# Cosine attention with a cosine MLP on one core: another order for the AV matmuls, a second DMA queue at the start, larger weight loads, and a refitted DMA model in the planner

## The chip, the cores and the metric

The kernel runs on one core of a Trainium2 chip. The metric is the device time of one execution in microseconds (us). Before the change the median of three runs was 438.87 us (437.8 to 439.41). The span in a profile is about 1.8 us shorter than the time of the same run.

Names used below: PE is the matmul engine, ACT the engine of exp, cosine and logarithm, DVE the vector engine, POOL the general engine, SP the engine that only issues DMAs. A bank is a piece of the memory in which PE adds up its results. A load lands when its last data have arrived. The granted clock is the share of PE's full speed that the profile records.

## The reference, cut to what matters

```python
# q, k, v: 8 batches x 12 heads x 448 x 64, float32; tau 0.1
q_n = q / (norm(q) + 1e-6);  k_n = k / (norm(k) + 1e-6)
attn = softmax(q_n @ k_n.T / tau)
x = (attn @ v) -> [3584, 768]           # heads side by side
h = x @ w_in                            # 768 x 2048, "M1" below
out = (h * cos(h)) @ w_out              # 2048 x 768, "M2" below
```

## The kernel before

Two heads make a pair. A batch has 6 pairs, a unit is 3 pairs, so there are 48 pairs, 16 units and 8 batches. In each pair PE forms scores (SC), ACT takes their exponential (PX), PE multiplies by v (AV), DVE divides. After six pairs M1 of the batch runs (96 matmuls of 448 columns), ACT takes the cosine (by a sine with an offset), DVE multiplies (gT), and M2 of that batch is left over as a reserve: its matmuls are placed one by one into PE's waits during the attention of the next batch. Where there is nothing to place, filler matmuls on zeros keep PE's clock up.

The order of the instructions on each engine is not written by hand. The program lists all operations with costs and dependencies, and a planner plays them through a model of the engines and of the DMA, tries 12 settings, and fixes each engine's order at build time. At run time each engine executes its list strictly in order. So a wrong number in the planner's model does no harm to the result; it gives an order that fits the chip badly.

The AV matmuls of a pair, before. `AVv[:, a]` are two banks, one for each head `a`; four chunks `c` of keys are added up in one target:

```python
def av(e, a):
    for x in range(NJ):                      # 4 groups of 112 queries
        k = a * S + NP * x
        for c in range(NJ):                  # 4 chunks, same target
            t = e.matmul(AVv[:, a, DV*x : DV*x + n], PXv[j][:, c, k : k + 128],
                         vav[i][:, NJ*(2*p + a) + c, 0:n], start=(c == 0), stop=(c == NJ - 1))
for a in range(2):                           # head after head
    P.op("PE", lambda e, a=a: av(e, a), ..., cost=NJ * NJ * 0.0324, ...)
```

The planner's choice between the attention's next group (at time `s`) and a waiting M2 matmul (at time `t`). `hold` is one of the settings that are tried, 0.1 or 0.2 us:

```python
if s is None or switched(t, o) < s - self.hold:
    s, c = t, (t, o, fill)                   # place M2 here
```

The planner's DMA model gives each load a bulk time and, where several queues are busy, shares the engines in proportion to a packet time:

```python
dma(eng, ..., "load u%d p%d", bulk = 0.82 per pair,  packet 0.055)   # q, k
dma("SP", ..., "load v",      bulk = 2.4,            packet 0.055)
dma("POOL", ..., "W1", 4 loads, bulk = 4.2 each,     packet 0.09)
dma("POOL", ..., "W2", 4 loads, bulk = 4.2 each,     packet 0.13)
```

## Time and profile before

| what | value |
|---|---|
| time | 438.87 us |
| span of the profile | 436.6 us |
| PE busy (filler included) | 97% |
| M1 of batch 0 starts | 37.84 us |
| M1 of batch 1 starts | 95.16 us |
| M1 of batches 2 to 5 start | 148.42, 196.88, 245.35, 293.81 us, every 48.47 us |
| last matmul starts | 432.03 us |

The starts of M1 are read from single matmuls in the trace. They cut the run into stages. The Trainium skill, "Perfetto Trace Analysis", says at its start that matmul busy time is a bad measure of how near a kernel is to its limit, because matmuls are pipelined. Here too the share misleads, if for other reasons: 97% includes 66 filler matmuls, and the first stages have waits that the share does not show.

These are the head, the DMA slices, the chain's share by engine, the AV group, and the issues of W1 from the page of the kernel before. A group has line, engine, operation, output from input, shapes, count, then busy us and mean ns of one (which includes the latency), then the idle time before it.

```profile
span 436.6 us, 8807 instructions
PE 423.0 (97%) x3774; PEld 230.6 (53%) x3774; DVE 211.8 (49%) x295; ACT 266.3 (61%) x320; POOL 191.6 (44%) x119
DMA  8999999899838296747948493848758101210222
...
PE 86%; ACT 5%; POOL 3%; DVE 2%; DMA 2%; SPq 1%; issue 0%; ACTq 0%; POOLq 0%
...
L782 PE MATMUL AV<-va,PX 112*128 112x65 bf16 x1536 | 57.2, 193 | 1.1 <-ACT PX L765 0.8
...
W<-in_moe_w_in_dram POOLq DMA_DIRECT2D x4, 768.0 KB, 12.1
```

The chain is PE for 86% of the span. L782 are the AV matmuls, 57.2 us for 48 pairs. The DMA is busy for 80% or more in each of the first eleven of forty slices, that is for the first 120 us.

PE's timeline (start, length, line, operation, count, idle time before) in the stage after M1 of batch 0 of the kernel before:

```profile
58.39 0.55 PE L760 MATMUL SC<-qkT 64*128 64x448 bf16 x4
58.87 2.12 PE L874 MATMUL PO<-W,gT 128*128 128x384 bf16 x12
60.83 0.54 PE L909 MATMUL PO<-zt 128*128 128x448 bf16 x2
61.84 0.36 PE L760 MATMUL SC<-qkT 64*128 64x448 bf16 x2 [0.47 <-ACT PX L765]
...
66.17 0.55 PE L909 MATMUL PO<-zt 128*128 128x448 bf16 x2
66.56 0.81 PE L874 MATMUL PO<-W,gT 128*128 128x384 bf16 x4
```

From 60.83 to 66.56 us there is no M2 (PO<-W,gT): PE runs scores and filler (L909). Further below this stretch is called the hole. The last W2 load landed at 60.87 us, and the planner had placed M2 after 65.20 us because its model expected the landing then. (Times that the planner expected are read from it when the kernel is built.)

### The profile page before, as it was taken

What the parts mean: (1) busy time and instruction counts of PE and PEld (TensorE: products, weight loads), DVE (VectorE), ACT (ScalarE), POOL (GpSimd) and SP (SyncE); (2) the same over time, 40 slices, a digit from 0 to 9 for tenths busy, and PEclk for the clock granted to TensorE, in tenths of its full rate; (3) what the DMA queues carried; (4) which work ended last, traced back from release to release, by engine and by line L of the source; (5) the groups of instructions that cost most, each with busy time, mean ns of one, the idle gap of its engine ahead of it and who ended that gap; (6) DMA issues with size and microseconds to landing.
All of it is one profiled execution on the core that took longest, in us unless ns stands there. A gap on an engine that the chain in (4) does not pass through costs nothing.

```text
span 436.6 us, 8807 instructions
## 1 busy us (share of the span) xinstructions
PE 423.0 (97%) x3774; PEld 230.6 (53%) x3774; DVE 211.8 (49%) x295; ACT 266.3 (61%) x320; POOL 191.6 (44%) x119
## 2 busy tenths in 40 slices
PE   8789989999999999999999999999999999999996
PEld 3455536555555555555555555555555555555663
DVE  4775644555752269233853268333852343244321
ACT  4886577774777646775487747774577647734000
POOL 0994347857594137910695048911695000000000
PEclk9999999999999999999999999999999999999999
DMA  8999999899838296747948493848758101210222
GB/s 211 247 230 209 239 244 196 196 211 249 224 80 163 62 263 158 135 99 187 240 64 153 114 270 80 167 112 200 180 101 146 46 0 48 69 38 2 73 74 72
DMA packets 95975, 63.87 MB, mean 146 GB/s; under 512 B 54976, under 2 KB 92352, under 8 KB 95936
## 3 DMA queue, kind: packets, MB, share of 16 engines
q1 hardware_dynamic: 90688, 57.02, 57.3%
q0 software_dynamic: 5248, 6.29, 8.3%
q8 instruction: 30, 0.49, 0.5%
q14 instruction: 9, 0.07, 0.1%
HBM read 45.61 MB, written 11.01 MB: 130 GB/s over the span
## 4 chain that ended last, share of the span: by engine, by line
PE 86%; ACT 5%; POOL 3%; DVE 2%; DMA 2%; SPq 1%; issue 0%; ACTq 0%; POOLq 0%
PE PO L874 30%; PE SC L823 20%; PE AV L823 12%; PE AV L782 11%; PE SC L760 9%; ACT PX L765 3%; PE SC L874 2%; DMA raw<-in_q_dram 2%; POOL qks L720 1%; POOL sq L694 1%; DVE n L701 1%; ACT cosb L837 1%; ACT sq L690 1%; PE AV L874 1%; ACT L613 1%; SPq L647 1%
## 5 line engine op out<-in xcount | busy, mean ns | idle before, releaser
L765 ACT ACTIVATE PX<-SC 112x896 bf16<-112x896 f32 x192 | 165.2, 914 | 44.5 <-PE SC L760 43.3
L874 PE MATMUL PO<-W,gT 128*128 128x384 bf16 x816 | 150.2, 326 | 0.0
L694 POOL TENSOR_TENSOR sq<-raw 112x1024 bf16<-112x1024 f32 x41 | 76.7, 1894 | 95.5 <-DMA raw<-in_q_dram 95.5
L874 PEld LDWEIGHTS PO<-W,gT 128*128 128x128 bf16 x816 | 72.9, 98 | 59.2 <-issue 13.0
L720 POOL TENSOR_TENSOR qks<-raw,rn 112x1024 bf16<-112x1024 f32 x47 | 88.3, 1902 | 23.3 <-ACT rn L712 23.2
L823 PE MATMUL SC<-xT,W 128*128 128x448 bf16 x480 | 95.4, 352 | 0.8 <-DVE gT L839 0.5
L839 DVE TENSOR_TENSOR gT<-SC,cosb 128x896 bf16<-128x896 f32 x40 | 43.6, 1091 | 59.5 <-ACT cosb L837 58.9
L837 ACT ACTIVATE cosb<-SC,cst 128x896 f32<-128x896 f32 x40 | 40.2, 1007 | 48.6 <-PE SC L823 46.2
L823 PEld LDWEIGHTS SC<-xT,W 128*128 128x128 bf16 x480 | 46.6, 98 | 43.8 <-issue 0.8
L701 DVE TENSOR_REDUCE n<-sq 112x16 f32<-112x1024 bf16 (+1 forms) x49 | 58.0, 1190 | 16.5 <-ACT sq L690 9.4
L782 PEld LDWEIGHTS AV<-va,PX 112*128 112x128 bf16 x1536 | 51.9, 97 | 15.9 <-issue 11.2
L823 PE MATMUL AV<-xT,W 128*128 128x448 bf16 x288 | 58.7, 352 | 0.1
L760 PE MATMUL SC<-qkT 64*128 64x448 bf16 x384 | 55.0, 355 | 3.8 <-ACT PX L765 1.4
L782 PE MATMUL AV<-va,PX 112*128 112x65 bf16 x1536 | 57.2, 193 | 1.1 <-ACT PX L765 0.8
L881 DVE COPY osb<-PO 128x384 f32<-128x384 f32 x51 | 28.1, 552 | 34.7 <-PE PO L874 34.7
L837 ACT ACTIVATE cosb<-AV,cst 128x896 f32<-128x896 f32 x24 | 24.2, 1007 | 33.1 <-PE AV L823 32.7
L791 DVE RECIPROCAL rcp<-AV 112x8 f32<-112x8 f32 x48 | 9.9, 206 | 67.7 <-PE AV L782 67.6
L823 PEld LDWEIGHTS AV<-xT,W 128*128 128x128 bf16 x288 | 28.0, 98 | 26.2 <-issue 0.5
L839 DVE TENSOR_TENSOR gT<-AV,cosb 128x896 bf16<-128x896 f32 x24 | 26.2, 1091 | 18.3 <-ACT cosb L837 17.9
L792 DVE TENSOR_TENSOR xs<-AV,rcp 112x512 bf16<-112x512 f32 x48 | 33.2, 691 | 2.0
L668 POOL CAST va<-vin 112x1536 bf16<-112x1536 f32 x14 | 20.5, 1462 | 26.1 <-PE AV L782 24.2
L760 PEld LDWEIGHTS SC<-qkT 64*128 64x128 bf16 x384 | 12.9, 93 | 34.9 <-ACT PX L765 17.5
(34 smaller groups left out, 130.9 us busy)
## 6 DMA issues: line engine op xcount, KB each, us to landing
vin<-in_v_dram SPq DMA_DIRECT2D x16, 672.0 KB, 10.4
raw<-in_k_dram SPq DMA_DIRECT2D x13, 672.0 KB, 6.8
raw<-in_q_dram SPq DMA_DIRECT2D x13, 672.0 KB, 8.7
W<-in_moe_w_in_dram POOLq DMA_DIRECT2D x4, 768.0 KB, 12.1
W<-in_moe_w_out_dram POOLq DMA_DIRECT2D x4, 768.0 KB, 19.2
out_dram<-osb SPq DMA_DIRECT2D x8, 336.0 KB, 3.1
out_dram<-osb SPq DMA_DIRECT2D x8, 288.0 KB, 2.7
raw<-in_k_dram SPq DMA_DIRECT2D x9, 224.0 KB, 8.2
```

Source lines behind the costliest of these rows:

```text
L694: pool(lambda e, x=x, y=y: e.tensor_tensor(y, x, x, ALU.mult), src_, dst, 0.1 + n * 1.78e-3, label="sq%d.%d" % (u, p))
L701: dve(lambda e, w=w: e.tensor_reduce(out=n2v[i][:, 2 * p : 2 * p + 2, w], in_=sqv[p][:, :, w, :], axis=mybir.AxisListType.X, op=ALU.add), ...
L720: f = lambda e, s0=s0, s1=s1: e.tensor_tensor(qksv[i][:, p, s0:s1, :, :].rearrange("p s h d -> p h s d"), rawv[i][:, h, s0:s1, :], bass.AP ...
L760: t = e.matmul(SCv[z][:, a, 0:S], qkT[k].ap()[r, NP * c : NP * c + 128], qkT[k].ap()[r, S : 2 * S], start=True, stop=True)
L765: act(lambda e: e.activation(PXv[j][:, c, 0 : 2 * S].rearrange("p (a s) -> p a s", a=2), SCv[z][0:NP, :, 0:S], ACT.Exp, scale=1.0 / TAU), ...
L782: t = e.matmul(AVv[:, a, DV * x : DV * x + n], PXv[j][:, c, k : k + 128], vav[i][:, NJ * (2 * p + a) + c, 0:n], start=(c == 0), stop=(c == ...
L792: dve(lambda e: e.tensor_tensor(xsv[y].rearrange("p x h d -> p h x d"), AXv[:, :, :, 0:D], bass.AP(rcp[y], 0, [[NS, NP], [NJ, 2], [1, NJ], ...
L823: t = e.matmul(ph[:, a, 0:S], W1v[:, c, 128 * n : 128 * n + 128], xTv[b % 2][:, c, :], start=(c == 0), stop=(c == NKC - 1))
L837: act(lambda e, ph=ph, cz=cz: e.activation(cosv[cz], ph[:, :, 0:S], ACT.Sin, bias=cst.ap()[:, 0:1], scale=1.0), names(gi) + ["cst0"], [("c ...
L839: dve(lambda e, ph=ph, cz=cz, gi=gi: e.tensor_tensor(gTv[:, 2 * gi : 2 * gi + 2, S * (b % 2) : S * (b % 2) + S], ph[:, :, 0:S], cosv[cz], ...
L874: r = e.matmul(po[:, 0:HW], gTv[:, y, col : col + 128], W2v[:, y, HW * hf : HW * hf + HW], start=(y == 0), stop=(y == NF - 1))
L881: dve(lambda e, po=po, o=o, hf=hf: e.tensor_copy(osb[o].ap()[:, HW * hf : HW * hf + HW], po[:, 0:HW]), keys, [("osb", o, hf)], HW, label=" ...
```

## The change

Its intent: the matmuls of AV should not wait for the accumulation before them; q, k and v of the first unit should arrive earlier; W1 should cost less DMA time; unit 5's load and norms should not delay batch 1; the planner should know the true landings. The diff, cut to its core (left out among others: new issue times for the weight loads, and the table load on ACT now behind the first issues of q):

```diff
-    "sq": ["AD", "A", "A", "P", "P", "P"],          # who squares: A = ACT, P = POOL, D = DVE
-    "scale": ["D", "P", "P", "P", "P", "P"],
+    "sq": ["AD", "A", "P", "P", "P", "P"],
+    "scale": ["DD", "P", "P", "P", "P", "P"],       # first pair by halves
...
+    MIXED = 0.9                                     # in the DMA model
-            turn = sum(o.pkt for o in run)
+            turn = sum(o.pkt for o in run) * (self.MIXED if len(run) > 1 else 1.0)
...
+            eng = "ACT" if u in HALF and x == (1,) else "SP"      # HALF = (0,): q of unit 0
-                "raw...", 0.82 * (p1 - p0) * len(x), ..., 0.055)
+                "raw...", 0.95 * (p1 - p0) * len(x), ..., 0.068)
...
+        views = (TPv, POv if apart else TPv)        # first pair: halves turned in two banks
...
-        def av(e, a):
-            for x in range(NJ):
-                for c in range(NJ):
+        def av(e, x0):
+            for x in range(x0, x0 + 2):
+                for c in range(NJ):
+                    for a in range(2):              # heads, so banks, alternate
...
-    NQ = 4                          # W1 bulk 4.2, packet 0.09; W2 bulk 4.2, packet 0.13
+    NQ1, NQ2 = 2, 4                 # W1 bulk 15.2 / 2, packet 0.079; W2 bulk 15.2 / 4, packet 0.119
...
-        if u == 3 and p == 1:
-            load(5, 0, UP)
+        if u == 3 and p == 2:
+            for x in range(UP):
+                load(5, x, x + 1)                   # after the store of pair 8's x
...
+            if g in DEFER:                          # DEFER = (2 * PB,): unit 5's norms after M1
+                norms(g // UP + 1, 0)
...                                                  # the last store: two queues, SP and ACT
```

Alternating heads is allowed because the two heads lie in two banks. The Trainium skill, "PSUM — Partial Sum Buffer", The four PSUM rules, says that the first matmul of an accumulation clears the written-bits of the whole bank, in the partitions that it writes; two sums begun in turns in one bank would spoil each other.

More of the change, by code (lines that the diff above doesn't have):

```diff
@@ L309, in transfer @@
                     continue
-                turn = sum(h[0].pkt for h in run)
+                turn = sum(h[0].pkt for h in run) * (self.MIXED if len(run) > 1 else 1.0)
                 step = min([h[2] * turn / h[0].pkt for h in run] + [stop - clock[0]])
@@ L517, in bass_cosine_attention__then__act_gcu_kernel @@
     NO = 4
-    DUE = (-20.0, 8.0, 12.0, 16.0, 20.0, 24.0, 28.0, 32.0)
+    DEFER = (2 * PB,)
+    VDVE = (0, 1)
+    HALF = (0,)
+    DUE = (-20.0, 10.0, 20.0, 24.0, 28.0, 32.0)
     LAG = 1
@@ L573, in bass_cosine_attention__then__act_gcu_kernel @@
     TPv = PO2.ap().bitcast(BF16)
+    POv = PO.ap().bitcast(BF16)
     vav = [t.ap().rearrange("p (x d) -> p x d", d=DV) for t in va]
@@ L635, in bass_cosine_attention__then__act_gcu_kernel @@
         pool(lambda e, i=i: e.memset(PXv[i][:, :, 2 * S :], 0.0), (), [("PX", i, c) for c in range(NJ)], 0.2, label="pad")
-    table(EXPSET)
     def src(t, u, h0, nh):
@@ L640, in src, with load @@
         return bass.AP(t.tensor, (b * NH + hb) * S * D, [[NJ * D, NP], [S * D, nh], [1, NJ * D]])
-    pooled, loads = [None], []
-    def load(u, p0, p1, apart=False, eng="SP", behind=None):
+    pooled, loads, quick = [None], [], []
+    def load(u, p0, p1, apart=False):
         i = u % 2
@@ L650, in load, with load_v @@
         for x in ((0,), (1,)) if apart else ((0, 1),):
-            behind = pooled[0] if eng == "POOL" else loads[-1] if loads else None
+            eng = "ACT" if u in HALF and x == (1,) else "SP"
+            behind = quick[-1] if eng == "ACT" and quick else None if eng == "ACT" or not loads else loads[-1]
             dma(eng, [f[y] for y in x], (), [("raw", i, p, y) for p in range(p0, p1) for y in x],
-                "raw%d_%d_%s%s" % (i, p0, x, eng), 0.82 * (p1 - p0) * len(x), "load u%d p%d" % (u, p0), behind, 0.055)
-            loads.append(P.ops[-1])
-            if eng == "POOL":
-                pooled[0] = P.ops[-1]
-    def load_v(u, eng="SP"):
-        i = u % 2
-        before = loads[-1] if loads and eng == "SP" else None
-        loads.append(dma(eng, [lambda e: e.dma_start(vin[i].ap().rearrange("p (h c) -> p h c", h=UH), src(v, u, 0, UH))],
-            (), [("vin", i)], "vin%d%s" % (i, eng), 2.4, "load v u%d" % u, pooled[0] if eng == "POOL" else before, 0.055))
-        if eng == "POOL":
-            pooled[0] = P.ops[-1]
+                "raw%d_%d_%s%s" % (i, p0, x, eng), 0.95 * (p1 - p0) * len(x), "load u%d p%d" % (u, p0), behind, 0.068)
+            (quick if eng == "ACT" else loads).append(P.ops[-1])
+    def load_v(u):
+        i = u % 2
+        loads.append(dma("SP", [lambda e: e.dma_start(vin[i].ap().rearrange("p (h c) -> p h c", h=UH), src(v, u, 0, UH))],
+            (), [("vin", i)], "vin%d" % i, 2.85, "load v u%d" % u, loads[-1], 0.068))
     def copy_v(u):
@@ L668, in copy_v @@
         f = lambda e: e.tensor_copy(vav[i][:, :, 0:D], vinv[i])
-        if u < 2:
+        if u in VDVE:
             dve(lambda e: e.tensor_reduce(
@@ L676, in halves @@
     def halves(parts):
-        if len(parts) == 1 or parts[0] == parts[1]:
-            return [(parts[0], (0, 1))]
+        if len(parts) == 1:
+            return [(parts, (0, 1))]
         return [(parts[0], (0,)), (parts[1], (1,))]
@@ L739, in transposes, with half @@
             return
-        def half(e, s0, s1):
+        views = (TPv, POv if apart else TPv)
+        keys = (("TP", 0), "PO" if apart else ("TP", 1))
+        def half(e, s0, s1, view):
             for s in range(s0, s1):
-                r = e.transpose(TPv[:, NP * s : NP * s + NP], qksv[i][:, p, s, :, :], ident.ap())
+                r = e.transpose(view[:, NP * s : NP * s + NP], qksv[i][:, p, s, :, :], ident.ap())
             return r
         for t in range(2):
-            P.op("PE", lambda e, t=t: half(e, NJ * t, NJ * t + NJ), [("qks", i, p, t), "ident"],
-                 [("TP", t)], cost=NJ * 0.0487, mode="F", label="TP%d" % g)
+            P.op("PE", lambda e, t=t: half(e, NJ * t, NJ * t + NJ, views[t]), [("qks", i, p, t), "ident"],
+                 [keys[t]], cost=NJ * 0.0487, mode="F", label="TP%d" % g)
         for t in ((0,), (1,)) if apart else ((0, 1),):
             w = slice(S * t[0], S * t[-1] + S)
-            dve(lambda e, w=w: e.tensor_copy(qkT[j].ap()[:, w], TPv[:, w]), [("TP", z) for z in t],
+            dve(lambda e, w=w, view=views[t[-1]]: e.tensor_copy(qkT[j].ap()[:, w], view[:, w]), [keys[z] for z in t],
                 [("qkT", j, z) for z in t], len(t) * S / 2, label="qkT%d" % g)
@@ L776, in attend @@
         i, b, n = u % 2, g // PB, D + 1
-        def av(e, a):
-            for x in range(NJ):
-                k = a * S + NP * x
+        def av(e, x0):
+            for x in range(x0, x0 + 2):
                 for c in range(NJ):
-                    t = e.matmul(AVv[:, a, DV * x : DV * x + n], PXv[j][:, c, k : k + 128],
-                                 vav[i][:, NJ * (2 * p + a) + c, 0:n], start=(c == 0), stop=(c == NJ - 1))
+                    for a in range(2):
+                        k = a * S + NP * x
+                        t = e.matmul(AVv[:, a, DV * x : DV * x + n], PXv[j][:, c, k : k + 128],
+                                     vav[i][:, NJ * (2 * p + a) + c, 0:n], start=(c == 0), stop=(c == NJ - 1))
             return t
         P.group = len(P.ops)
-        for a in range(2):
-            P.op("PE", lambda e, a=a: av(e, a), [("va", i)] + [("PX", j, c) for c in range(NJ)], ["AV"],
-                 cost=NJ * NJ * 0.0324, mode="F", label="AV%d" % g)
+        for x0 in range(0, NJ, 2):
+            P.op("PE", lambda e, x0=x0: av(e, x0), [("va", i)] + [("PX", j, c) for c in range(NJ)], ["AV"],
+                 cost=NJ * NJ * 0.0300, mode="F", label="AV%d" % g)
         P.group = None
@@ L825, in f @@
                 return t
-            P.op("PE", f, [("W1", n // 4)] + [("xT", b % 2, c) for c in range(c0, c1)], names(gi), cost=(c1 - c0) * MM,
+            P.op("PE", f, [("W1", n * NQ1 // NF)] + [("xT", b % 2, c) for c in range(c0, c1)], names(gi), cost=(c1 - c0) * MM,
                  mode="F", label="M1 %d.%d" % (b, n))
@@ L876, in go @@
                     return r
-                P.op("PE", go, [("W2", f // 4)] + sorted({("gT", x, y // 2) for y in range(f, f + step) for x in par}),
+                P.op("PE", go, [("W2", f * NQ2 // NF)] + sorted({("gT", x, y // 2) for y in range(f, f + step) for x in par}),
                      keys, cost=step * MH, mode="F", label="M2 %d" % t, stream="B")
@@ L882, in m2_emit @@
                 keys, [("osb", o, hf)], HW, label="osb%d" % t)
-            if hf == 1:
-                sg = segments(t)
+            sg = segments(t)
+            if t == B * S // 128 - 1:
+                for x, (p0, cnt, row) in enumerate(sg):
+                    w = slice(HW * hf, HW * hf + HW)
+                    q = ("SP", "ACT")[x % 2 if hf else 0]
+                    dma(q, [lambda e, p0=p0, cnt=cnt, row=row, o=o, w=w: e.dma_start(
+                        bass.AP(out.tensor, row * DM + w.start, [[NJ * DM, cnt], [1, HW]]), osb[o].ap()[p0 : p0 + cnt, w])],
+                        [("osb", o, hf)], [], "last%s" % q, 0.6, "out%d" % t, None, 0.14)
+            elif hf == 1:
                 dma("SP", [lambda e, p0=p0, cnt=cnt, row=row, o=o: e.dma_start(
@@ L896, in load_w1 @@
     def load_w1(x):
-        w = FF // NQ
+        w = FF // NQ1
         pooled[0] = dma("POOL", [lambda e: e.dma_start(
             W1v[:, :, w * x : w * x + w], bass.AP(moe_w_in.tensor, w * x, [[FF, 128], [128 * FF, NKC], [1, w]]))],
-            (), [("W1", x)], "W1_%d" % x, 4.2, "W1.%d" % x, pooled[0], 0.09, 1000.0 + DUE[x])
+            (), [("W1", x)], "W1_%d" % x, 15.2 / NQ1, "W1.%d" % x, pooled[0], 0.079, 1000.0 + DUE[x])
     def load_w2(x):
-        w = NF // NQ
+        w = NF // NQ2
         pooled[0] = dma("POOL", [lambda e: e.dma_start(
             W2v[:, w * x : w * x + w, :], moe_w_out[128 * w * x : 128 * w * (x + 1), :].rearrange("(f p) n -> p f n", p=128))],
-            (), [("W2", x)], "W2_%d" % x, 4.2, "W2.%d" % x, pooled[0], 0.13, 1000.0 + DUE[4 + x])
+            (), [("W2", x)], "W2_%d" % x, 15.2 / NQ2, "W2.%d" % x, pooled[0], 0.119, 1000.0 + DUE[NQ1 + x])
     zero = dve(lambda e: e.memset(zt.ap(), 0.0), (), ["zt"], S)
@@ L912, in bass_cosine_attention__then__act_gcu_kernel @@
     for g in range(PB):
-        load(g // UP, g % UP, g % UP + 1, g == 0)
+        load(g // UP, g % UP, g % UP + 1, g == 0 or g // UP in HALF)
         if g % UP == UP - 1:
             load_v(g // UP)
+    table(EXPSET)
+    for y in quick:
+        P.order_only(y, P.ops[-1])
     def find(label):
@@ L943, in pair @@
         u, p = g // UP, g % UP
-        if p == 0 and u >= 2 and u + 1 < NU:
+        if p == 0 and u >= 2 and u + 1 < NU and g not in DEFER:
             norms(u + 1, 0)
@@ L953, in pair @@
                 load_v(4)
-        if u == 3 and p == 1:
-            load(5, 0, UP)
+        if u == 3 and p == 2:
+            for x in range(UP):
+                load(5, x, x + 1)
+            P.order_only(find("X8"), P.ops[-3])
             load_v(5)
@@ L960, in pair @@
             grouped(transposes, g + 1)
-        if BYPE <= g + 3 < NG:
+        if BYPE <= g + 3 < NG and g not in DEFER:
             transposes(g + 3)
@@ L965, in bass_cosine_attention__then__act_gcu_kernel @@
     norms(0, 0)
-    transposes(0)
+    transposes(0, True)
     norms(0, 1)
@@ L969, in bass_cosine_attention__then__act_gcu_kernel @@
     P.order_only(find("scale0.0"), find("red0.1"))
+    for y in [o for o in P.ops if o.label == "qkT0"]:
+        P.order_only(y, find("red0.1"))
     load_w1(0)
@@ L978, in bass_cosine_attention__then__act_gcu_kernel @@
         load(2, p, p + 1)
-    load_w1(2)
-    load_w1(3)
     load_w2(0)
@@ L984, in bass_cosine_attention__then__act_gcu_kernel @@
     load(3, 0, UP)
-    after(P.ops[-1], find("W1.3"))
+    after(P.ops[-1], find("W1.%d" % (NQ1 - 1)))
     load_v(2)
@@ L1007, in bass_cosine_attention__then__act_gcu_kernel @@
             m1(points[g])
+            if g in DEFER:
+                norms(g // UP + 1, 0)
+                transposes(g + 3)
             first = [o for o in P.ops[first:] if o.eng == "PE"][0]
@@ L1023, in bass_cosine_attention__then__act_gcu_kernel @@
     P.arrange()
-    P.emit(nc, ["out%d" % o for o in range(NO)])
+    P.emit(nc, ["out%d" % o for o in range(NO)] + ["lastSP", "lastACT"])
     ctx.close()
```

## The prediction

> What bounds the kernel now. The page of the profile gives PE 97% busy, but part of that is filler (L909). In the chain of waits six batches from 148.6 us on repeat every 48.4 us (148.58, 197.04, 245.51, 293.98, 342.44 us) with almost no piece that is not PE. So from about 116 us to 432 us PE is the limit. Before that it is not. The slices show DMA at 80 to 99% for about 98 us.
>
> Three stages before the steady part, from PE's timeline:
> - 0 to 37.8 us, attention of batch 0. The chain of waits runs through q's landing (9.82 us), a square on ACT (9.84 to 10.9), then POOL without a pause from 11.5 to 24.6 us.
> - 37.8 to 58.4 us, first half of the MLP of batch 0: 96 matmuls x 0.189 = 18.1 us of work in 20.6 us.
> - 58.4 to 95.2 us, attention of batch 1 and M2 of batch 0: by my count about 28 us of PE work in 36.8 us. Between 60.8 and 66.6 us PE runs pairs of score matmuls and filler, and waits for ACT. Yet the last W2 load had landed at 60.87 us (DMA issues with landings). M2 was placed later because the planner's old model expects W2 later: 4.2 x (1 + 0.055/0.13) = 6.0 us per contended load, where the trace shows about 5.4.
>
> What the change does:
> 1. AV order. Starts of single matmuls in the trace: 32 to 33 ns inside an accumulation of four, 29 ns at each change of target. The Trainium skill, "TensorE: Matmul & The Clock Gate", Back-to-back issue gap, gives N/2.4 + 2.5 = 29.6 ns for N = 65 and no wait for accumulating onto the same address; the trace has that wait, about 3.4 ns. Alternating heads alternates banks, so all should be near 29.5. 24 x 3.4 ns = 0.08 us a pair, 3.9 us for 48 pairs, about 3.4 us on the critical path.
> 2. Start. The second square leaves ACT for POOL, idle until 11.5 us; ln and rn come about 0.7 us earlier; one W1 issue (0.8 us) leaves POOL's chain. 1 to 2 us at the start of M1. q of pairs on ACT's queue shares the same 16 engines (the skill, "Trainium Kernel Development and Optimization", Key Constraints), so it saves only issue time, below 0.5 us.
> 3. W1 in two loads doubles its packets. Packets of 1024 bytes took 97 ns, of W2's 1536 bytes 135 ns: 10.5 against 11.4 bytes/ns. My estimate: 1.5 us less DMA time before W2 lands.
> 4. The refit (5.4 us per contended load: 3.8 x (1 + 0.068/0.119) x 0.9) puts M2 into the hole at 61 to 66 us: 3 to 4 us. With 2 and 3, M1 of batch 1 starts at 89.5 instead of 95.2 us.
> 5. Later unit 5 and deferred norms take a 0.95 us square and a 1.2 us reduce out of the chain at 90 to 93 us: about 0.5 us net.
> 6. The last store split over two queues: 0.5 us of the 4.2 us after the last matmul.
>
> Sum: 5.7 + 3.0 (AV after 95 us) + 0.5 + 0.5 = 9.7 us; I take off a tenth for reordering losses. Predicted 430.0 us, range 426.0 to 435.0. Chances: faster by over 2% 0.50, within 2% 0.48, slower 0.02.
>
> Right if: AV groups of 32 take 0.95 us; batch period 47.9 us; filler at 61 to 66 us gone; M1 of batch 1 at about 90 us.
>
> Wrong if: 29 ns cannot be sustained with a weight load for each matmul; unit 3's norms (POOL scale until 79 us) keep batch 1 late; POOL's added square delays its chain; the plan meets other landings than it assumes.

## The result, and the profile after

The changed kernel took 433.01 us (median of four runs, 432.25 to 434.07) against 438.9 us of the kernel before. The ratio is 0.9871, with a 95% interval from 0.9841 to 0.9901. A ratio here is the mean time of one kernel's fast runs over that of the other's in the same rounds, so it isn't quite the ratio of the medians. The time is inside the predicted range and within 2%. The outputs are right.

A second measurement of the same kernel (a_again below) gave 435.09 us and 0.9893. It was run at another time. The medians of the kernel before were within 0.6 us (438.77 to 439.3), its single runs between 437.38 and 441.79 us. So the 2 us between the two medians of the changed kernel need a reason, and one is shown below.

The lines of the page after that answer to those above:

```profile
span 430.4 us, 8767 instructions
PE 417.9 (97%) x3756; PEld 225.6 (52%) x3756; DVE 213.2 (50%) x297; ACT 264.5 (61%) x319; POOL 192.7 (45%) x118
...
PE 81%; ACT 6%; DMA 6%; POOL 4%; issue 1%; DVE 1%; SPq 1%; ACTq 0%
...
L785 PE MATMUL AV<-va,PX 112*128 112x65 bf16 x1536 | 54.7, 193 | 0.8 <-ACT PX L767 0.8
...
W<-in_moe_w_in_dram POOLq DMA_DIRECT2D x2, 1536.0 KB, 14.9
```

AV fell from 57.2 to 54.7 us, and W1 comes in two loads of double size. The chain is less of PE (81% for 86%) and more of DMA (6% for 2%). Three pieces of the chain of the changed kernel, in order of time (start, length, what), show where the DMA got into it:

```profile
113.57 7.50 POOL qks L719 x4
...
123.24 8.12 DMA raw<-in_q_dram
131.43 3.75 POOL sq L693 x2
```

Loads of q and k and what POOL makes of them now decide something in batch 1. In the kernel before, the chain from 116.50 us to the end of that batch is PE alone.

The stages, from the starts of M1 and of the last matmul, with the number of M2 matmuls that lie in each:

| stage | before, us | M2 | after, us | M2 | difference |
|---|---|---|---|---|---|
| up to M1 of batch 0 | 37.84 | 0 | 36.52 | 0 | -1.32 |
| M1 of 0 to M1 of 1 | 57.31 | 96 | 53.74 | 96 | -3.57 |
| M1 of 1 to M1 of 2 | 53.26 | 116 | 52.67 | 116 | -0.59 |
| M1 of 2 to M1 of 3 | 48.47 | 104 | 48.73 | 104 | +0.26 |
| M1 of 3 to M1 of 6 | 3 x 48.47 | 3 x 104 | 3 x 47.77 | 3 x 100 | -2.10 |
| M1 of 6 to M1 of 7 | 39.31 | 76 | 38.72 | 72 | -0.59 |
| M1 of 7 to last matmul | 50.44 | 192 | 52.97 | 208 | +2.53 |
| last matmul to the end of the span | 4.6 | | 3.7 | | -0.8 |

The table has a trap. From M1 of batch 3 on three stages are 0.70 us shorter and the next is 0.59 us shorter, which looks like a full success of the new AV order. But each has four M2 matmuls less, and one takes 0.1625 us (4 matmuls take 0.65 us), and these 16 matmuls are done at the end, in the stage that became 2.53 us longer. For the stretch from M1 of 3 to the last matmul the sum is -0.16 us. The 23 AV groups in that stretch should have given 23 x 48 ns = 1.1 us. So nearly the whole gain, 4.9 of about 6 us, came before M1 of batch 1.

The hole after the change, on PE's timeline:

```profile
58.88 0.54 PE L919 MATMUL PO<-zt 128*128 128x448 bf16 x2
60.21 0.36 PE L762 MATMUL SC<-qkT 64*128 64x448 bf16 x2 [0.79 <-ACT PX L767]
...
62.12 0.82 PE L877 MATMUL PO<-W,gT 128*128 128x384 bf16 x4
```

The hole is 3.2 us long now (58.88 to 62.12) instead of 5.7 us. The last W2 load landed at 58.41 us, and v of unit 2 at 60.90 us, where the new model expected 60.76 and 61.16 us. The refit is not what shortened the hole: a_oldmodel (experiment 6) has one of the same length with the old numbers.

### The profile page after: what moved, and what is told of

The parts are those of the page before. It is cut to its first block, busy times and chain, and to the rows that moved or that the text cites. A ratio compares the mean times of both kernels' runs of the same rounds, so it can differ in the third digit from the quotient of the medians.

```text
span 430.4 us, 8767 instructions
## 1 busy us (share of the span) xinstructions
PE 417.9 (97%) x3756; PEld 225.6 (52%) x3756; DVE 213.2 (50%) x297; ACT 264.5 (61%) x319; POOL 192.7 (45%) x118
## 4 chain that ended last, share of the span: by engine, by line
PE 81%; ACT 6%; DMA 6%; POOL 4%; issue 1%; DVE 1%; SPq 1%; ACTq 0%
PE PO L877 28%; PE SC L826 20%; PE AV L826 12%; PE AV L785 10%; PE SC L762 8%; ACT PX L767 5%; DMA raw<-in_q_dram 4%; PE SC L877 2%; POOL qks L719 2%; DMA vin<-in_v_dram 2%; POOL sq L693 1%; PE AV L877 1%; ACT L618 1%; PE PO L745 0%; ACT cosb L840 0%
## 5 line engine op out<-in xcount | busy, mean ns | idle before, releaser
L877 PE MATMUL PO<-W,gT 128*128 128x384 bf16 x816 | 148.6, 326 | 0.0
L693 POOL TENSOR_TENSOR sq<-raw 112x1024 bf16<-112x1024 f32 x42 | 79.3, 1903 | 101.9 <-DMA raw<-in_q_dram 101.9
L719 POOL TENSOR_TENSOR qks<-raw,rn 112x1024 bf16<-112x1024 f32 x47 | 88.4, 1903 | 25.1 <-ACT rn L711 25.1
L842 DVE TENSOR_TENSOR gT<-SC,cosb 128x896 bf16<-128x896 f32 x40 | 43.6, 1091 | 55.2 <-ACT cosb L840 54.7
L785 PEld LDWEIGHTS AV<-va,PX 112*128 112x128 bf16 x1536 | 49.4, 97 | 15.5 <-issue 11.4
L785 PE MATMUL AV<-va,PX 112*128 112x65 bf16 x1536 | 54.7, 193 | 0.8 <-ACT PX L767 0.8
L842 DVE TENSOR_TENSOR gT<-AV,cosb 128x896 bf16<-128x896 f32 x24 | 26.2, 1091 | 18.9 <-ACT cosb L840 18.7
```

Of the source, the lines that this page charges most:

```text
L693: pool(lambda e, x=x, y=y: e.tensor_tensor(y, x, x, ALU.mult), src_, dst, 0.1 + n * 1.78e-3, label="sq%d.%d" % (u, p))
L719: f = lambda e, s0=s0, s1=s1: e.tensor_tensor(qksv[i][:, p, s0:s1, :, :].rearrange("p s h d -> p h s d"), rawv[i][:, h, s0:s1, :], bass.AP ...
L785: t = e.matmul(AVv[:, a, DV * x : DV * x + n], PXv[j][:, c, k : k + 128], vav[i][:, NJ * (2 * p + a) + c, 0:n], start=(c == 0), stop=(c == ...
L842: dve(lambda e, ph=ph, cz=cz, gi=gi: e.tensor_tensor(gTv[:, 2 * gi : 2 * gi + 2, S * (b % 2) : S * (b % 2) + S], ph[:, :, 0:S], cosv[cz], ...
L877: r = e.matmul(po[:, 0:HW], gTv[:, y, col : col + 128], W2v[:, y, HW * hf : HW * hf + HW], start=(y == 0), stop=(y == NF - 1))
```

## The experiments

Twelve runs were made: eleven edited kernels, and the changed kernel again. The kernel before took 438.98, 439.3 and 438.77 us in them. "Same plan" means that the order of all the other instructions was kept. Letters in the texts name theories; the sentence ahead of each says what is asked.

### 1. The AV order

The theory after the result was that the new order saves 48 ns a pair and no more, since that is what the trace of the changed kernel has; the prediction had 82 ns. Mean distances between the starts of the matmuls of one group, in ns, from the single matmuls of the trace:

```
before, 4 targets:   32.4 32.3 29.1 | 33.0 32.1 32.5 29.1 | 32.9 32.1 32.9 29.2 | 32.7 32.3 32.4 29.1   first to last 995 ns
changed:             29.2 29.1 29.2 31.7 | 29.1 29.2 29.2 34.1 | 29.2 29.2 29.1 31.7 | 29.2 29.1 29.2 34.2   first to last 947 ns
```

(Of the 31 distances, the 3rd to the 17th are shown before, and the last 16 after the change.) Before, the three steps inside a sum are 32 to 33 ns and the step to the next target is 29 ns. That step stays in the same bank most of the time, so a change of bank isn't needed; the address of the target fits. It is not isolated, because at the same step the weights come from another place too. Nor is the wait general: M1 too adds six matmuls up on one address, and its steps, of 448 columns, are 189 ns inside a sum and to the next target alike. After the change most of the last 16 steps are 29 ns, but each fourth is 32 or 34 ns, at places where nothing in the data suggests it.

b_av is the kernel before with the new AV order alone, same plan:

```diff
-        def av(e, a):
-            for x in range(NJ):
+        def av(e, x0):
+            for x in range(x0, x0 + 2):
                 for c in range(NJ):
+                    for a in range(2):
...
```

> The kernel before with one edit: the order of the attention-value matmuls is that of the changed kernel; plan, order of all other work and every engine's sequence stay (the planner's cost is kept, the plans were compared). The after trace has starts of 29 ns with 32 to 34 ns at about every fourth, 947 ns from first to last of a group against 995. Theory A (saving is 48 ns a group and PE is the limit from 66 us on): 42 groups x 48 ns = 2.0 us faster, ratio 0.995, M1 period 48.2 us instead of 48.47. Rival B (the full 82 ns a group of the prediction, lost in the changed kernel to its other plan): 3.5 us faster, ratio 0.992. Rival C (the order alone is worth nothing): ratio 1.000.

Measured: 437.38 us, ratio 0.9957 [0.9932, 0.9983]. Group first to last: 947 ns. The stage of a batch is 48.15 us with 104 M2, where the kernel before has 48.47 us with as many. So the order alone is worth about 0.3 us a batch, and its interval agrees with 48 pairs x 48 ns = 2.3 us; theory B's 0.992 and theory C's 1.000 lie outside it.

a_av_back is the changed kernel with the old AV order, same plan:

> The changed kernel with the old order of the attention-value matmuls, same plan on every engine. Theory A: 48 ns x 36 to 42 groups, 1.7 to 2.0 us slower than the changed kernel (about 434.9 us), ratio to before 0.991. Rival B: 3.5 us slower. Rival C: no difference, ratio 0.987.

Measured: 437.02 us, ratio 0.9944 [0.9918, 0.9970]; the steady stage is 48.08 us with 100 M2 against 47.77 us, so 0.31 us a batch. Both ways round the order is worth 48 ns a group. In total it is 2 us (against the repeat, by ratios) to 4 us (against the first measurement, by medians) slower than the changed kernel; the order explains 2.3 us of that, and the rest is within what the changed plan varies by (experiment 5).

a_seq takes the chunks as 0, 2, 1, 3 and leaves all else. If the long fourth step hung on a chunk or an address, it should move; if it goes with the count of instructions, it should stay.

> The changed kernel with the four chunks of each attention-value sum in the order 0, 2, 1, 3 instead of 0, 1, 2, 3; heads still alternate, plan the same. In the changed kernel the start of every fourth matmul came 32 to 34 ns after the one before, the others 29 ns; from the sixteenth on these were the second heads of chunks 1 and 3. Theory R (it goes with the data: the second head's odd chunks): the long steps become neighbours, the sixth and eighth matmul of each eight. Rival S (it goes with the count of instructions, whatever they read): every fourth stays long. Either way about 947 ns from first to last, correct.

Measured, in one look without timed rounds: 436.39 us, results correct, first to last 947.3 ns, and each fourth step still long (32.3 and 33.3 ns). So the step doesn't go with the chunk's address. What makes it is open; that it is the supply of instructions is only a guess.

### 2. Why the shorter AV did not shorten the batches

PE's timeline at the end of M1 of batch 3, kernel before, then the changed kernel (SC and AV here are banks in which M1 forms h):

```profile
210.50 2.43 PE L823 MATMUL SC<-xT,W 128*128 128x448 bf16 x12
212.77 0.81 PE L874 MATMUL PO<-W,gT 128*128 128x384 bf16 x4
213.42 0.92 PE L823 MATMUL AV<-xT,W 128*128 128x448 bf16 x4
```

```profile
205.28 2.43 PE L826 MATMUL SC<-xT,W 128*128 128x448 bf16 x12
207.82 0.92 PE L826 MATMUL AV<-xT,W 128*128 128x448 bf16 x4
```

Before, the 12 + 4 matmuls fill the time exactly: 12 x 0.189 + 4 x 0.1625 = 2.92 us, from 210.50 to 213.42. After the change the four M2 matmuls are gone, and from 205.28 to 207.82 there are 2.54 us for 2.27 us of work: PE waits 0.27 us for DVE to free the bank. The planner's best trial, read at build time, had hold 0.1 before and 0.2 after. With 0.2 it does not put M2 into so small a wait. It thought this plan the best by its own model, and it costs nearly what the AV order saves in a batch (0.29 us).

a_fill takes hold 0.1 from 100 us on. (In a_fill, a_fill2 and a_w2m the planner plans anew, and its other settings are held at those that the changed kernel's best trial had.)

```diff
-                if s is None or switched(t, o) < s - self.hold:
+                if s is None or switched(t, o) < s - (self.hold if t < 100.0 else 0.1):
```

> The changed kernel with one edit in its planner: from 100 us on an M2 piece may be put in where it saves 0.1 us, not 0.2 us. The plan is the same up to 105 us and has four M2 matmuls before the last group of each M1 again, as the kernel before had. Theory D (the changed kernel gives back 0.26 us in each of seven M1 stages because PE stands idle there): PE period from M1 to M1 48.2 us with 104 M2 matmuls in it instead of 47.77 with 100, 1.5 to 1.8 us faster than the changed kernel, about 431.4 us, ratio to before 0.983. Rival E (the idle time only moves elsewhere, since the wait is for DVE and ACT): no difference, 0.987.

Measured: 434.29 us, ratio 0.9878 [0.9852, 0.9904], so no gain in total. The steady stage was as expected, 48.15 us with 104 M2, which is 0.27 us less for the same work. But the plan of batch 1 became different too, and it waited 1.0 us for gT at 114.65 us and 0.84 us at 163.09 us. Whether the edit made these waits is open: the unedited kernel, run again, had one of 1.30 us too (experiment 5).

a_fill2 therefore does it only from 146 us on, after batch 1:

> As a_fill, but the smaller threshold holds only from 146 us on, so that batch 1 keeps the changed kernel's plan. In a_fill the steady period was 48.15 us with 104 M2 matmuls against 47.77 with 100, which is 0.27 us less for the same work (four M2 are 0.65 us), but the batch before took 1.5 us longer with a 1 us wait for gT. Theory D: the plan's four M2 matmuls in M1's wait are worth 0.27 us for each batch from 3 to 7, 1.1 to 1.4 us faster than the changed kernel of the same call, ratio to before 0.984. Rival E (same): 0.987.

Measured: 431.87 us (430.78 to 434.2), ratio 0.9841 [0.9811, 0.9871]. The profile has M2 back in its place:

```profile
205.56 2.43 PE L826 MATMUL SC<-xT,W 128*128 128x448 bf16 x12
207.83 0.81 PE L877 MATMUL PO<-W,gT 128*128 128x384 bf16 x4
208.48 2.43 PE L826 MATMUL AV<-xT,W 128*128 128x448 bf16 x12
```

The stage is 48.15 us with 104 M2 and the last one has 192 M2. This is the lowest median of all: against the changed kernel (435.09 us) it is 3.2 us lower, by the ratios 2.3 us. The intervals of the two ratios overlap by a little there, and widely with that of the first measurement (0.9871), so a gain over the changed kernel is likely, not sure. The filled wait explains about 1.1 to 1.4 us of that (0.27 us in four or five stages). For the rest, the profile of a_fill2 shows no long wait for gT in batches 1 and 2, and that may be chance (experiment 5).

### 3. The second queue at the start

a_qsp is the changed kernel with q of the first unit issued by SP again, same plan. The prediction gave the queue under 0.5 us; the rival was that it is worth more, because v and the third pair come earlier.

```diff
+    sp = [o for o in P.ops if o.label in ("load u0 p0", "load u0 p1", "load u0 p2") and o.eng == "SP"]
+    for y, z in zip(quick, sp):                     # after the planner has fixed the order
+        y.eng, y.start = "SP", z.start + 0.01
...                                                 # and ACT no longer waits for these issues
```

> The changed kernel with the three q loads of the first unit back on SP's queue, each behind its k load; the plan is the same on every engine otherwise. Theory F (two queues share the same 16 DMA engines; the second queue saves issue time only): first pair lands within 0.5 us of the changed kernel's 4.75 us, M1 of batch 0 starts at 36.5 to 37.0 us, total within 0.5 us of the changed kernel. Rival G (two queues move more bytes per us, as the refitted model says with its factor 0.9): third pair and v land about 0.8 us later, M1 of batch 0 starts at 37.3 us or later.

Measured: 435.21 us (six runs; 435.06 us without the slow one), ratio 0.9908 [0.9881, 0.9936]. M1 of batch 0 starts at 39.23 instead of 36.52 us (37.12 us in the changed kernel's repeat). In total a_qsp is 0.7 to 1.6 us slower than the changed kernel by the ratios, and the intervals overlap. The DMA windows from 3 to 6 us, changed kernel, then a_qsp (packets, bytes, rate):

```profile
DMA packets 1009, 0.96 MB, mean 322 GB/s; under 512 B 67, under 2 KB 1009, under 8 KB 1009
```

```profile
DMA packets 775, 0.75 MB, mean 249 GB/s; under 512 B 47, under 2 KB 775, under 8 KB 775
```

So two queues moved more bytes a microsecond through the same engines in this window. All profiles agree: 292 to 329 GB/s in the eleven with two queues, 246 to 257 in the three with one. But the window flatters, as one queue moved more before 3 us: from 1.5 to 6 us it is 242 to 256 against 230 to 240 GB/s. The third pair of q landed at 8.03 us instead of 9.53 (8.62 in the repeat), v at 10.61 instead of 12.25 (11.22). Their issues on SP and ACT had ended 1.43 and 1.50 us earlier as well, since the seven loads were issued on two engines, at about 0.5 us each, and not all on SP. So issue time alone can account for the landings; how much the higher rate adds is open. The first q even landed later with two queues, at 4.75 instead of 4.20 us. POOL's timeline shows why that matters. The changed kernel, then a_qsp:

```profile
8.18 2.27 POOL L693 TENSOR_TENSOR sq<-raw 112x1024 bf16<-112x1024 f32 x1 [6.73 <-DMA raw<-in_q_dram]
10.91 1.02 POOL L908 DMA_DIRECT2D W<-in_moe_w_in_dram  x1 [0.46 <-DMA vin<-in_v_dram]
11.96 3.77 POOL L719 TENSOR_TENSOR qks<-raw,rn 112x1024 bf16<-112x1024 f32 x2
```

```profile
9.68 1.89 POOL L693 TENSOR_TENSOR sq<-raw 112x1024 bf16<-112x1024 f32 x1 [8.23 <-DMA raw<-in_q_dram]
12.55 1.02 POOL L908 DMA_DIRECT2D W<-in_moe_w_in_dram  x1 [0.98 <-DMA vin<-in_v_dram]
13.60 3.77 POOL L719 TENSOR_TENSOR qks<-raw,rn 112x1024 bf16<-112x1024 f32 x2
```

POOL works in order, and its first W1 issue is made to wait for v. With v 1.64 us later, the issue and the scaling of pairs 2 and 3 (L719) are 1.64 us later, and that is the chain to M1. The rest of the 2.7 us is PE's clock, on PE's timeline of a_qsp, then of the changed kernel:

```profile
15.57 0.57 PE L745 MATMUL PO<-ident,qks 112*128 112x112 bf16 x8 [2.48 <-POOL qks L719]
15.97 1.81 PE L785 MATMUL AV<-va,PX 112*128 112x65 bf16 x32
17.72 0.93 PE L762 MATMUL SC<-qkT 64*128 64x448 bf16 x4
```

```profile
13.93 0.57 PE L745 MATMUL PO<-ident,qks 112*128 112x112 bf16 x8 [0.28 <-POOL qks L719]
14.33 1.13 PE L785 MATMUL AV<-va,PX 112*128 112x65 bf16 x32
15.39 0.55 PE L762 MATMUL SC<-qkT 64*128 64x448 bf16 x4
```

After 2.48 us without work the same 32 matmuls took 1.81 instead of 1.13 us. The Trainium skill, "TensorE: Matmul & The Clock Gate", Part 1, says that PE's clock halves after an idle window of about 3.4 us; the trace agrees in kind, and shows it after a shorter wait. Its record of the granted clock is 0.5 from 16.14 to 19.56 us, and in the 3.41 us before that PE was busy for 0.93 us. This plan was made for earlier landings, so a plan made for one queue could lose less. The kernel before, with its own plan and one queue, started M1 at 37.84 us.

### 4. The square, W1's packets and the hole

a_sqact gives the third pair's square back to ACT, as before the change, all else the same:

```diff
-    "sq": ["AD", "A", "P", "P", "P", "P"],
+    "sq": ["AD", "A", "A", "P", "P", "P"],
```

> The changed kernel with the square of the third pair on ACT again, as before; every other engine's order is the same. Theory L (the prediction's: the square leaves ACT, so ln, rn and POOL's chain come 0.7 us or more earlier): POOL's first scale 0.7 us or more later than in the changed kernel (11.96 us, 12.6 in the repeat), M1 of batch 0 later by as much. Rival M (rn of the second pair waits for DVE's reduce at 9.5 to 10.7 us and POOL's first scale for the W1 issue that waits for v's landing, so where the square runs is of no account): POOL's first scale within 0.3 us of v's landing plus 1.3 us, M1 of batch 0 at 36.5 to 37.1 us, total as the changed kernel.

Measured: 433.77 us, ratio 0.9889 [0.9857, 0.9922]; M1 of batch 0 at 36.88 us. That is 0.36 us later than in the profile of the changed kernel, and earlier than in its repeat (37.12 us). The place of the square is of no account.

a_w1four loads each half of W1 by two DMAs with rows of 1024 bytes, same plan:

> The changed kernel with each half of W1 loaded by two DMAs of half the columns, so packets of 1024 bytes instead of 2048; plan, landing conditions and every engine's order stay. Theory J (the prediction's: bigger packets carry more bytes per ns): W1's packets take 97 ns per 1024 bytes instead of 175 ns per 2048, 18.7 us of 16-engine time instead of 16.8; W1 lands 1 to 1.5 us later than 38.0 us, the last W2 lands near 60 us instead of 58.4, M1 of batch 1 starts 0 to 1.5 us later, total 0 to 1.5 us slower than the changed kernel. Rival K (other queues fill the time, packets' size does not count): landings within 0.3 us, total the same. POOL pays about 0.8 us more for each extra issue in either case.

Measured: 434.67 us, ratio 0.9892 [0.9859, 0.9925], the same as the unedited kernel (435.09, 0.9893). The packets were as expected: 97 ns for 1024 bytes, 18.7 us of 16 engines' time for W1, against 175 ns for 2048 bytes and 16.8 us. But W1 had landed at 39.17 us against 39.61 us in the repeat and 38.04 us in the first profile. M1 of batch 0 was later by 1.2 us (38.33 against 37.12), since POOL issues twice more, and that was made good by M1 of batch 2. The prediction's 1.5 us of DMA time is there in the records (1.9 us), but no run shows it in the time.

a_w2m asks what filling the hole is worth. It takes the planner's safety margin away for the W2 loads only, so that M2 is placed at the expected landing:

```diff
-                        if o.start > 5.0:
+                        if o.start > 5.0 and not o.label.startswith("W2"):
```

> The changed kernel, planner without its safety margin for W2's landings alone: the model then has the last W2 at 57.8 us (it landed at 58.4), so M2 follows it at once and the filler at 58.9 to 62.1 us is replaced by M2. Theory H (the prediction's: the hole is lost time, filling it is worth 1.5 to 3 us): M1 of batch 1 starts at 87.5 to 89 us, total 1.5 to 2.5 us faster than the changed kernel. Rival I (batch 1's pairs are held by norms and exps; M2 done early is missing later as something to do while they are awaited): M1 of batch 1 starts at 90.3 us or later (up to 93.5), filler or idle time moves to 80 to 93 us, total the same or up to 3 us slower.

Measured: 435.81 us, ratio 0.9921 [0.9885, 0.9957]. PE's timeline of a_w2m shows the hole filled:

```profile
59.61 0.82 PE L877 MATMUL PO<-W,gT 128*128 128x384 bf16 x4 [0.40 <-DMA W<-in_moe_w_out_dram]
60.36 0.36 PE L762 MATMUL SC<-qkT 64*128 64x448 bf16 x2
60.66 0.82 PE L877 MATMUL PO<-W,gT 128*128 128x384 bf16 x4
```

And yet M1 of batch 1 starts at 93.92 us, 3.7 us later than in the changed kernel (2.3 us later than in its repeat). The stage has the same 96 M2 matmuls, and 16 filler matmuls instead of 6: the M2 that filled the hole were missing later, where PE then waited. M2 is a reserve. Spent in one wait it is not there for the next, and in this plan it gained nothing to spend it early. The plan differs in more than the hole, though: unit 5's loads were issued from 76.88 to 79.51 us instead of 79.53 to 87.96, and the planner itself reckoned with M1 of batch 1 at 93.7 instead of 90.5 us. So the run shows that filling the hole is not enough, not that it is worth nothing in any plan.

### 5. The spread of the changed kernel

a_again is the changed kernel, unedited, in the second call:

> The changed kernel once more, unedited, as the yardstick for the runs of the same call and for how much its profile varies. Expected: 433 us, ratio to before 0.987; M1 of batch 0 at 36.5 us, of batch 1 at 90.3 us, of batch 2 at 143 to 144 us (the one stretch that differed by up to 1 us between profiles of the same plan).

Measured: 435.09 us (432.98 to 435.65), ratio 0.9893 [0.9865, 0.9921]. The stage from M1 of 1 to M1 of 2 took 53.99 us, not 52.67. PE's and then DVE's timeline of this run:

```profile
110.10 0.36 PE L762 MATMUL SC<-qkT 64*128 64x448 bf16 x2
111.76 0.36 PE L762 MATMUL SC<-qkT 64*128 64x448 bf16 x2 [1.30 <-DVE gT L842]
```

```profile
109.40 1.22 DVE L700 TENSOR_REDUCE n<-sq 112x16 f32<-112x1024 bf16 x1 [1.80 <-POOL sq L693]
110.53 1.08 DVE L842 TENSOR_TENSOR gT<-SC,cosb 128x896 bf16<-128x896 f32 x1
```

The order on DVE is fixed: the reduce of unit 6's squares stands before the gT that frees a bank for PE. Unit 6's q landed at 107.40 us here and at 104.20 us in the first profile. POOL squared it at once (107.47 us), DVE waited 1.80 us for that square with gT behind it in its list, and PE waited 1.30 us. With the earlier landing there was no such wait. (Of the 3.2 us, 1.3 us are M1 of batch 1, which itself started later here. The planner had expected the landing at 103.44 us.) So the order that the planner fixed turns a late DMA into a wait of PE, through two engines which were idle.

### 6. The refit

a_oldmodel is the changed kernel with the planner's old DMA numbers; nothing else is undone:

```diff
-    MIXED = 0.9
+    MIXED = 1.0
-  raw 0.95 / 0.068   v 2.85 / 0.068   W1 15.2 / NQ1, 0.079   W2 15.2 / NQ2, 0.119
+  raw 0.82 / 0.055   v 2.4  / 0.055   W1 16.8 / NQ1, 0.09    W2 16.8 / NQ2, 0.13
```

> The changed kernel with the planner's DMA numbers of before and no factor for mixed queues; code and loads stay, the plan differs. The model then has the last W2 at 64.3 us (it landed at 58.4 to 59.5). Theory N (the refit's worth is the shorter hole after M1 of batch 0): hole at the start of batch 1 longer by 2 to 3 us, M1 of batch 1 at 92 to 94 us instead of 90.3 to 91.6, total 1.5 to 2.5 us slower than the changed kernel (ratio 0.994 to 0.995 against 0.987 to 0.989). Rival O (pairs and their norms set batch 1's end, as the run without W2's margin showed, so the hole's length is of no account): M1 of batch 1 within 0.7 us of the changed kernel's, same total.

(The diff is shortened to the numbers.) Measured: 440.52 us (438.82 to 444.33), ratio 1.0046 [0.9983, 1.0110]. All other parts of the change together, without the refit, show no gain. By the medians the refit is worth 5.4 us (against the repeat) to 7.5 us (against the first measurement) in this plan. Part of it is PE's clock: the two runs with a mean granted clock of 1.0 and 0.999 took 438.82 and 439.35 us, the two with 0.996 and 0.991 took 441.69 and 444.33 us. The loss isn't where the prediction looked for it, in the hole: that is 3.2 us long (61.84 to 65.07), as in the changed kernel, where 2 to 3 us more were expected. M1 of batch 1 is at 93.18 us, 2.9 us later than in the first profile and 1.6 us later than in the repeat, and most of the loss is in the stage after it, which takes 57.46 us with 112 M2 (52.67 and 53.99 us with 116). PE's timeline, then DVE's:

```profile
113.00 0.36 PE L762 MATMUL SC<-qkT 64*128 64x448 bf16 x2
116.10 0.36 PE L762 MATMUL SC<-qkT 64*128 64x448 bf16 x2 [2.73 <-DVE gT L842]
...
118.22 1.70 PE L785 MATMUL AV<-va,PX 112*128 112x65 bf16 x32 [0.81 <-ACT rn L711]
```

```profile
111.88 1.22 DVE L700 TENSOR_REDUCE n<-sq 112x16 f32<-112x1024 bf16 x1 [2.69 <-POOL sq L693]
113.73 1.22 DVE L700 TENSOR_REDUCE n<-sq 112x16 f32<-112x1024 bf16 x1 [0.63 <-POOL sq L693]
114.87 1.08 DVE L842 TENSOR_TENSOR gT<-SC,cosb 128x896 bf16<-128x896 f32 x1
```

It is the wait of experiment 5, with two reduces ahead of gT. Unit 6's loads landed at 109.88 us, where the planner had expected 105.36 us; the order only works if they come earlier. PE waits 2.73 us, and the next 32 AV matmuls take 1.70 us at the lowered clock (0.5 from 118.52 to 121.93 us). A share of the later stages is lost too (49.40 us for one steady stage, with two waits for ACT), so not every microsecond of the loss is located.

### 7. Unit 5's load and norms

a_nodefer puts unit 5's load one pair earlier again, in one piece, and doesn't put its norms off:

```diff
-    DEFER = (2 * PB,)
+    DEFER = ()
-        if u == 3 and p == 2:
-            for x in range(UP):
-                load(5, x, x + 1)
...
+        if u == 3 and p == 1:
+            load(5, 0, UP)
```

> The changed kernel with unit 5 loaded in one piece one pair earlier and its norms before batch 2's first pair, as before; planned anew. Theory P (the later unit 5 is worth 1 to 2 us at the end of batch 1, since a square and a reduce stood in its chain): M1 of batch 1 at 92 to 93 us, total 1 to 2 us slower than the changed kernel. Rival Q (what is gained there is lost in batches 1 and 2 by unit 6's and 7's later loads, for which DVE's reduce holds up gT by 0.3 to 1.5 us): M1 of batch 1 later by 1 to 2 us, but from there to M1 of batch 3 100.9 us or less against 101.4 to 103.3, total within 0.7 us of the changed kernel.

Measured: 435.14 us, ratio 0.9912 [0.9891, 0.9933]. M1 of batch 1 is at 92.43 us, 2.2 us later than in the first profile of the changed kernel and 0.9 us later than in its repeat, so the deferral does work there. But M1 of 1 to M1 of 3 takes 100.87 us against 101.40 us (103.30 us in the repeat): the norms that were put off have to be done in that stretch, so a part may come back as a cost. The 0.5 us are less than the 1.9 us by which the stretch differs between the two profiles of the changed kernel, so this isn't shown. In total 0.8 to 1.8 us separate it from the changed kernel by the ratios, and the intervals overlap, so the size in total stays open.

## Why the prediction was right or wrong

The total came into the range: 430.0 predicted, 433.0 and 435.1 us measured, inside the range the first time and just above its upper edge (435.0) the second. Of the 8.9 us of gain that were forecast, 3.0 us did not come (3.8 us in the repeat). That the sum came this near is partly luck: parts of it were wrong, and their errors had opposite signs. Of the prediction's four marks, the AV group (947 ns) and M1 of batch 1 (90.27 us) were met, the period of a batch was met by count only, and the filler in the hole was not gone.

| term of the sum | predicted | measured |
|---|---|---|
| M1 of batch 1 starts earlier | -5.7 us | -4.9 us (-3.6 in the repeat) |
| AV after that, with all else up to the last matmul | -3.0, and -0.5 for norms | -0.5 us (+1.6 in the repeat) |
| last store | -0.5 us | -0.8 us |

1. AV order. The part of the mechanism that was tested was right: the new order takes most of the 32 to 33 ns steps away (b_av, a_av_back). That they come from adding onto the address just written fits, but was not isolated. The size was off: 48 ns a group instead of 82, since each fourth step stays at 32 to 34 ns. And of the 0.29 us a batch that are left, the plan gave 0.27 us back by a wait in M1 that it no longer filled. This is the term that failed most; the prediction's batch of 47.9 us was met by 47.77 us, for the wrong reason, as the stage had lost four M2 matmuls.
2. Start. M1 came 1.3 us earlier, as predicted (1 to 2 us), or 0.7 us in the repeat; b_av, with the old start, had it at 37.17 us, so profiles differ by as much. It came not by the means named. The square is of no account (a_sqact). The queue on ACT was put below 0.5 us, and without it M1 of batch 0 is 2.7 us later in a fixed plan (2.1 us against the repeat), of which about 1.1 us is the halved clock. The prediction took from the skill, "Trainium Kernel Development and Optimization", Key Constraints, that issuing from several engines saves only the sequencer's issue time; the runs do not refute that, though the rate was higher too. The step that failed is the size, "below 0.5 us": the third pair's q and v were issued 1.43 and 1.50 us earlier, and landed 1.50 and 1.64 us earlier.
3. W1's packets: right in the records (97 ns for 1024 bytes, 175 ns for 2048), without effect on the time (a_w1four).
4. The refit: expected at 3 to 4 us, by filling the hole. It is worth 5.4 to 7.5 us by the medians (a_oldmodel), though the hole is 3.2 us long with the old numbers as with the new, and the one plan that filled it gained nothing (a_w2m). The step that failed is "puts M2 into the hole" as the source of the gain. What the profile of a_oldmodel shows in its place is the order on POOL and DVE around the landings in batch 1, where PE waited 2.73 us at once. The chance given to "the plan meets other landings than it assumes" was the right worry: a load of unit 6 that landed 3.2 us later cost PE 1.30 us (a_again).
5. Unit 5: worth 0.9 to 2.2 us at M1 of batch 1 instead of 0.5, part of which may come back in batches 1 and 2.
6. The last store: 0.8 us for 0.5; no run undid it alone.

That 12 AV groups lie before M1 of batch 1 and 36 after it also makes the first two rows of the table no clean separation of causes; the experiments are.

What stays open: the cause of the long fourth step; which part of the refit's gain lies outside batch 1, and how much of it another plan would keep; whether the target's address or the weights' place makes the 3.4 ns; the total of the deferral; and how the 1.3 us of the start divide between two queues and the halved first pair, which no run undid alone.

## What to carry to other kernels

When work is moved between stages, count the work in each stage before you call a shorter stage a gain: 0.70 us a batch here was 0.65 us put off. A reserve of independent matmuls is worth what the later waits are worth, so filling an early hole need not be a gain: here it was none. Where the order of engines is fixed at build time, the accuracy of the landing times in the model can be worth more than any single operation: an in-order engine that waits for a late load holds up what stands behind it.

## What the Trainium skill lacked or had wrong

- "TensorE: Matmul & The Clock Gate", Back-to-back issue gap: it has no wait for adding onto the address just written. The runs show 32 to 33 ns a step inside a sum against 29 ns otherwise (65 columns), which fits such a wait without isolating it; at 448 columns there is none. Nor has it the longer step of 32 to 34 ns at each fourth matmul.
- The same section calls N/2.4 + 2.5 ns the gap of isolated matmuls and gives other figures for streams with a weight load for each. Here such streams keep to the formula: 29 ns for 65 columns in most steps, 162.5 ns for 384 and 189 ns for 448.
- The same page, Part 1, names an idle window of about 3.4 us. Here 2.48 us of idle PE were followed by 32 AV matmuls in 1.81 instead of 1.13 us, and 2.73 us (then 0.81 us) by 1.70 us. Before the half clock began PE had been busy for 0.93 of 3.41 us in the first case and 1.61 of 3.52 us in the second, so the window need not be idle throughout.
- "Trainium Kernel Development and Optimization", Key Constraints, and "DMA: Bandwidth & Descriptors", Issuing engines are not separate DMA queues: both say that several issuing engines save only issue time. The runs do not refute that, but the saving was not small: v was issued 1.50 us earlier and landed 1.64 us earlier (1.03 in the repeat). That the rate from 1.5 to 6 us was higher too, 242 to 256 GB/s with two queues against 230 to 240 with one, neither page has.
